# First softmax times values: four 32-column tiles of the matmul array, one for each batch and head

## Chip, core and metric

The kernel runs on one core of one Trainium2 chip, in one launch. The time is device microseconds of one execution; of several executions the median counts. The engines are named as in the profile: PE is TensorE's matmul, PEld its load of the stationary operand, DVE is VectorE, ACT is ScalarE, POOL is GpSimd, SP is the queue that issues most DMAs.

## The reference

Inputs are float32. Batch 8, heads 8, sequence 576, head width 64, 32 packed rows. `A` is the attention with the packed rows; what follows is a channel mixing block and a second one.

```
def sm_attn(qq, kk, vv):
    s = scale * np.matmul(qq, kk.transpose(0, 1, 3, 2))
    s = s - np.max(s, axis=-1, keepdims=True)
    a = np.exp(s)
    a = a / (np.sum(a, axis=-1, keepdims=True) + 1e-09)
    return np.matmul(a, vv)
p_packed = sm_attn(p, k, v)          # 32 rows a head
out = sm_attn(q, p_packed, p_packed) # 576 rows a head
...
k = np.maximum(xk @ w_k, 0.0); v = k * k @ w_v        # xk, xr: x mixed with the row before
r = 1.0 / (1.0 + np.exp(-(xr @ w_r))); x = r * v
...
u = x + (xt @ U @ V).transpose(0, 2, 1); return u + np.maximum(u @ w_ch1, 0.0) @ w_ch2
```

The change lies in the product `a @ v` of the first softmax, the last line of `sm_attn` in its first call.

## The kernel before

Attention is cut into 16 units: a unit is two batches (`b2`) by two heads (`h`), so four pairs of batch and head with 32 packed rows each, 128 rows in all. `attention_steps` writes one unit. Keys are turned (`kin` to `kh`), the packed rows are turned (`pbd` to `pT`), scores go to PSUM, `Exp` writes the unnormed weights to `a1` (512 columns for the first 512 keys, and 128 columns, block diagonal by batch, for the last 64). `a1` is turned into `at`, whose columns are the 128 packed rows in the order batch, head, row. `at` is then the stationary operand and the values `vin` stream: that is the product of the change. `pp` (the STT on DVE at L262) multiplies the result by the reciprocal sum `st[:, 9:10]` and by `hmask`, which keeps for each row the 64 columns of its own head and puts 0 in those of the other. `pp` is turned into `ppt` for the second softmax and copied to `ppz` for the last product; `xo` goes to HBM (`x_d`).

Before the change the product streams both heads' 128 value columns past a stationary tile of 64 columns (one batch, two heads): for each of four tiles of keys two matmuls, `b2` = 0 and 1, into PSUM partitions 0 to 63 and 64 to 127. The last 64 keys of both batches are one full 128 by 128 matmul. That makes nine matmuls a unit; half of what they compute is masked away. A float32 matmul runs as two passes, each with its own weight load, so the trace has 18 loads and 18 matmuls for a unit.

The program is not written in the order in which it runs. Every operation is added to `Plan`, with the operations it depends on; `Plan.emit` then runs through a model of the engines and puts each operation into its engine's queue when the model has it ready, by class (`cls`; attention has 0, the main blocks 1, weight casts 0, 1 or 3) and then by order of writing (PE, SP) or by time ready (others). Where an operation may run on ACT or DVE (`copy`, `square`), the model's clocks choose. The model's cost of a matmul is set in `mm` (L197): `f * max(f * n / 2.4, 107.0) + 3.0` nanoseconds with `f` = 2 for float32 and `n` streamed columns. The order is thus fixed at build time, and the engines run their queues in it.

Units 0 to 3 run first, interleaved by `LAG`, while the weights `w_r` and `w_k` are cast to pairs of rounded parts (`Cast.run`: on DVE per 128 by 512 block four full-width steps on `st`, `a`, `m`, one full-width split and two at double rate). Then twelve chunks of 384 columns follow; the other twelve units run beside the first of them, until 477 us. A chunk mixes (`mix`: ACT `m`, DVE `m`, `xr` or `xk`), multiplies (`psr`, `psk`, `psv`), and squares (`sq`, `kk`). The last part, from 752 us on, is the second block (`psc`).

Of the kernel before, what the change touches and what calls it, by code (L numbers as in the profile page):

```python
# [469 lines left out]
def packed_attention_moe_mixer_kernel(  # L470
# [18 lines left out]
    B, H, S, D = q.shape  # L489
    NP = p.shape[2]  # L490
    P = 128
# [16 lines left out]
    plan = Plan(nc)  # L508
    add, sub, mul = ALU.add, ALU.subtract, ALU.mult
# [22 lines left out]
    def ctile(name, shape, dt=F32):  # L532
        return plan.fixed(const.tile(shape, dt, name=name))

    ident = ctile("ident", [P, P])
    hmask = ctile("hmask", [P, 2, D])
# [8 lines left out]
    def ps_att():  # L545
        return plan.bank(att_banks[0], "psat", att_banks[0] is ps_a)
# [87 lines left out]
    def attention_steps(A, u, u_next):  # L634
        bp, j = divmod(u, NJ)
        kin, qin, vin = A.kin.pop(u), A.qin.pop(u), A.vin.pop(u)
# [5 lines left out]
        qt, at = A.big(F32, "qt"), A.big(F32, "at")  # L642
# [11 lines left out]
        for b2 in range(2):  # L654
            yield
            ps = ps_att()
# [6 lines left out]
        ps = ps_att()  # L663
# [10 lines left out]
        st = plan.tile(A.one, [P, 16], F32, "st", parts=(0, 1))  # L674
        sps = []
        for c in range(2):
            yield
            ps = ps_att()
            for b2 in range(2):
                plan.mm(ps[b2 * 64:(b2 + 1) * 64, 0:288], pT[:, b2, :],  # L680
                        kh[:, b2 * 576 + c * 288:b2 * 576 + (c + 1) * 288],
                        start=True, stop=True, skip_group_check=True)
# [16 lines left out]
        for c in range(3):  # L699
            yield  # L700
            ps = ps_att()
# [13 lines left out]
        ps = ps_att()  # L715
# [4 lines left out]
        ps = ps_att()  # L720
# [2 lines left out]

        yield
        ps = ps_att()
        vm = vin[:, 0:1024].rearrange("p (b h t d) -> p b h t d", b=2, h=2, t=4)
        for t in range(4):
            for b2 in range(2):
                plan.mm(ps[b2 * 64:(b2 + 1) * 64, 0:P],
                        at[:, t * P + b2 * 64:t * P + (b2 + 1) * 64], vm[:, b2, :, t, :],  # L730
                        start=(t == 0), stop=False, skip_group_check=True)
        plan.mm(ps[:, 0:P], at[:, 512:640], vin[:, 1024:1152], start=False, stop=True, skip_group_check=True)
        pp = plan.tile(A.one, [P, P], F32, "pp")
        plan.stt(pp, ps[:, 0:P], st[:, 9:10], hmask.rearrange("p h d -> p (h d)"), mul, mul)
        plan.copy(ppz[:, 0, :], pp)
        if not plain:
            plan.tt(ppz[:, 1, :], pp, ppz[:, 0, :], sub)
# [3 lines left out]
        ps = ps_att()  # L741
# [36 lines left out]
        ps = ps_att()  # L778
# [4 lines left out]
        ps = ps_att()  # L783
# [5 lines left out]
        for c0, c1 in ((256, 576), (0, 256)):  # L789
# [4 lines left out]
            for n, (lh, rh) in enumerate(terms):  # L794
                for b2 in range(2):
                    r = slice(b2 * 64, (b2 + 1) * 64)
                    plan.mm(pss[b2][:, 0:w], ppz[r, lh, :], rh[r, c0:c1], start=(n == 0),
                            stop=(n + 1 == len(terms)))
# [5 lines left out]
    def attention(A, u, u_next):  # L804
        for _ in attention_steps(A, u, u_next):
            pass
# [94 lines left out]
    plan.cls = 0  # L901
    A0.after = go
    steps = [attention_steps(AX_[u], u, NJ if u == 0 else None) for u in range(NJ)]
    step = 0
    while any(s is not None for s in steps):
# [301 lines left out]
    def product(q, f, i, name, fresh):  # L1207

        if fresh:
            bank_abc[name] = plan.bank(ps_c1, "psc1")  # L1210
        ps = bank_abc[name][:, 0:256]
        w, x = load_ws(f, i), ops[q][i]
        n = 0
        for k in range(2):
            for wi, a in PASS:
                plan.mm(ps, half(w, wi)[:, k * P:(k + 1) * P],
                        half(x, a)[:, k * 256:(k + 1) * 256],
                        start=(fresh and n == 0), stop=(n == 5), skip_group_check=True)
                n += 1
        return ps  # L1220
# [53 lines left out]
    for n in range(len(chunks)):  # L1274
        b, c = chunks[n]
# [59 lines left out]
    for q in range(NQ):  # L1335
# [11 lines left out]
        for f in range(NF):  # L1347
# [7 lines left out]
            b = product(q, f, 1, "b", True)  # L1355
# [71 lines left out]
```

## Time and profile before

| | |
|---|---|
| median of 3 runs | 1553.74 us (1549.9 to 1557.67) |
| profiled execution | 1553.02 us |
| its span, first to last instruction | 1551.2 us |
| PE busy | 1506.0 us, 97% of the span |
| DVE, ACT busy | 964.3 us, 705.0 us |
| mean granted TensorE clock | 0.986 |

The profiled execution's own time is 1.8 us longer than its span, which covers what lies before the first and after the last instruction. A busy PE is not yet PE at its peak: matmul records overlap, so the time that a kind of matmul costs is read from the distance between starts and not from one record's length. A granted clock of 1.00 is the level of 2.4 GHz, 0.50 that of 1.2 GHz.

### The profile page before, as it was taken

How to read it: one execution, taken by the hardware profiler on the slowest of the kernel's cores; microseconds unless marked ns; L12 is line 12 of the kernel's file. 1: busy time of each engine (PE TensorE's matmuls, PEld its weight loads, DVE VectorE, ACT ScalarE, POOL GpSimd, SP SyncE). 2: the span in 40 equal slices, each digit the busy share in tenths (PEclk: the TensorE clock that was granted, in tenths of full speed). 3: DMA queues.
4: the chain of work that ended last, by engine and by line, in shares of the span. 5: the costliest groups of instructions: out<-in, count | busy, mean ns of one | idle time of the engine just before them, and what ended most of it. 6: DMA issues, size and time to landing. Idle time of an engine off the chain costs nothing.

```text
span 1551.2 us, 24711 instructions
## 1 busy us (share of the span) xinstructions
PE 1506.0 (97%) x8836; PEld 1311.0 (85%) x8836; DVE 964.3 (62%) x2227; ACT 705.0 (45%) x1627; POOL 270.6 (17%) x522
## 2 busy tenths in 40 slices
PE   6879899999999999999999999999999999999998
PEld 5658687888878888888899998989999999999997
DVE  5988977788887776787645354444545454443533
ACT  4867576666675666566532232222222222222221
POOL 0000000000000000001133333333333333333331
PEclk8898999999999999999999999999999999999999
DMA  9866546465554323657777867686866768676763
GB/s 200 202 175 168 155 106 170 126 184 163 158 155 142 125 92 128 240 181 241 234 211 188 215 169 224 163 239 155 234 165 180 212 168 226 162 217 157 204 171 101
DMA packets 226745, 275.59 MB, mean 178 GB/s; under 512 B 101696, under 2 KB 120448, under 8 KB 226624
## 3 DMA queue, kind: packets, MB, share of 16 engines
q0 software_dynamic: 72576, 132.15, 32.5%
q1 hardware_dynamic: 154048, 141.87, 31.5%
q8 instruction: 71, 1.16, 0.3%
q14 instruction: 50, 0.41, 0.1%
HBM read 221.45 MB, written 52.50 MB: 177 GB/s over the span
## 4 chain that ended last, share of the span: by engine, by line
PE 91%; DMA 4%; DVE 2%; ACT 2%; SPq 1%; issue 1%; DVEq 0%; ACTq 0%
PE psc L197 48%; PE psk L197 13%; PE psv L197 12%; PE psr L197 6%; PE psat L197 5%; PE psat L208 3%; SPq L311 1%; PE psu L197 1%; PE psh L197 1%; PE pst L208 1%; DMA s<-w_d 1%; DMA st<-in_moe_w_k_dram 1%; ACT a L229 1%; DMA qin<-in_q_dram 1%; DMA x_d<-xo 0%
## 5 line engine op out<-in xcount | busy, mean ns | idle before, releaser
L197 PE MATMUL psc<-w,hid 128*128 128x512 f32 x1728 | 446.5, 393 | 0.0
L197 PEld LDWEIGHTS psc<-ob,wb 128*128 128x128 f32 x3024 | 406.9, 190 | 28.3 <-ACT tmp L280 1.6
L197 PE MATMUL psc<-ob,wb 128*128 128x256 f32 x3024 | 420.9, 283 | 1.3 <-ACT tmp L280 1.3
L311 POOL DMA_DIRECT2D wb<-ws_d x504 | 267.2, 530 | 586.9 <-PE psc L197 489.7
L197 PEld LDWEIGHTS psc<-w,hid 128*128 128x128 f32 x1728 | 305.9, 189 | 50.2 <-ACT xu L280 0.2
L197 PE MATMUL psk<-xk,wk 128*128 128x384 f32 x1152 | 235.2, 345 | 1.7 <-DVE xk L250 0.9
L197 PE MATMUL psv<-wv,kk 128*128 128x512 f32 x864 | 226.8, 399 | 3.0 <-DVE wv L250 2.1
L250 DVE TENSOR_TENSOR tmp<-tmp,psc 128x256 f32<-128x256 f32 x288 | 120.7, 419 | 152.3 <-PE psc L197 141.4
L197 PEld LDWEIGHTS psk<-xk,wk 128*128 128x128 f32 x1152 | 202.6, 190 | 13.6 <-issue 3.7
L229 ACT ACTIVATE hid<-tmp 128x256 fp32r<-128x256 f32 x216 | 85.2, 416 | 248.9 <-DVE tmp L250 248.6
L197 PEld LDWEIGHTS psv<-wv,kk 128*128 128x128 f32 x864 | 157.9, 188 | 36.9 <-issue 2.8
L265 DVE SCALAR_TENSOR_TENSOR hid<-psc,hid 128x256 fp32r<-128x256 f32 x72 | 30.5, 424 | 186.4 <-ACT hid L229 186.4
L197 PE MATMUL psr<-wr,xr 128*128 128x512 f32 x432 | 111.4, 401 | 6.2 <-ACT r L280 3.0
L280 ACT ACTIVATE tmp<-psc 128x256 f32<-128x256 f32 x144 | 54.7, 380 | 137.8 <-PE psc L197 137.8
L303 POOL MEMSET x<- 128x8 f32 x4 | 0.8, 206 | 576.2 <-DVE m L262 392.0
L197 PEld LDWEIGHTS psr<-wr,xr 128*128 128x128 f32 x432 | 79.5, 189 | 25.7 <-ACT r L280 3.9
L265 DVE SCALAR_TENSOR_TENSOR hid<-tmp,hid 128x256 fp32r<-128x256 f32 x216 | 86.2, 421 | 18.0 <-ACT hid L229 12.9
L250 DVE TENSOR_TENSOR kk<-sq,kk 128x384 fp32r<-128x384 f32 x96 | 52.5, 553 | 45.3 <-ACT kk L280 43.7
L229 ACT ACTIVATE sq<-psk 128x384 f32<-128x384 f32 x96 | 46.5, 489 | 64.4 <-PE psk L197 63.4
L229 ACT ACTIVATE hid<-psc 128x256 fp32r<-128x256 f32 x72 | 27.5, 382 | 103.6 <-PE psc L197 103.6
L229 ACT ACTIVATE m<-x,om_t 128x384 f32<-128x384 f32 x96 | 57.2, 609 | 7.0 <-DVE xk L250 2.8
L262 DVE SCALAR_TENSOR_TENSOR m<-x,mu_t,m 128x384 f32<-128x384 f32 x96 | 57.9, 610 | 2.1 <-ACT m L229 1.7
(147 smaller groups left out, 1685.9 us busy)
## 6 DMA issues: line engine op xcount, KB each, us to landing
wb<-ws_d POOLq DMA_DIRECT2D x504, 256.0 KB, 3.1
st<-in_moe_w_ch_dram SPq DMA_DIRECT2D x32, 512.0 KB, 4.9
ws_d<-wb SPq DMA_DIRECT2D x56, 256.0 KB, 3.4
qin<-in_q_dram SPq DMA_DIRECT2D x32, 288.0 KB, 5.6
x_d<-xo SPq DMA_DIRECT2D x16, 576.0 KB, 3.4
x_d<-x SPq DMA_DIRECT2D x36, 256.0 KB, 3.7
u<-x_d SPq DMA_DIRECT2D x36, 256.0 KB, 5.5
out_dram<-u SPq DMA_DIRECT2D x36, 256.0 KB, 3.6
```

Of the source, the lines that this page charges most:

```text
L197: self.nc.tensor.matmul(o, l, r, start=start, stop=stop, **k)
L208: self.nc.tensor.transpose(out.get(), in_.get(), ident.get())
L229: self.nc.scalar.activation(o, in_.get(), func, **k)
L250: return self.elem(engs, lambda e, o, x, y: e.tensor_tensor(out=o, in0=x, in1=y, op=op), out, [a, b], self.TT, cls)
L262: ("dve",), lambda e, o, x, y, z: e.scalar_tensor_tensor(out=o, in0=x, scalar=z, in1=y, op0=op0, op1=op1), out, [a, b, s], {"dve": (1.042, ...
L265: ("dve",), lambda e, o, x, y: e.scalar_tensor_tensor(out=o, in0=x, scalar=s, in1=y, op0=op0, op1=op1), out, [a, b], self.TT, cls)
L280: self.nc.scalar.activation(o, i, AF.Copy)
L303: (self.nc.gpsimd if eng == "pool" else self.nc.vector).memset(o, 0.0)
L311: (self.nc.sync if eng == "sp" else self.nc.gpsimd).dma_start(out=o, in_=i)
```

## The change

The product is now 20 matmuls a unit: for each of five tiles of keys (`t`; the fifth is the last 64 keys of both batches) four matmuls, one for each pair of batch and head (`g`). The stationary operand is 32 columns of `at`, the streamed one the 64 value columns of that batch and head, and the result goes to 32 PSUM partitions and 64 columns. `pp` then reads the 64 columns twice, by a broadcast, and masks as before.

```
-        vm = vin[:, 0:1024].rearrange("p (b h t d) -> p b h t d", b=2, h=2, t=4)
-        for t in range(4):
-            for b2 in range(2):
-                plan.mm(ps[b2 * 64:(b2 + 1) * 64, 0:P],
-                        at[:, t * P + b2 * 64:t * P + (b2 + 1) * 64], vm[:, b2, :, t, :],
-                        start=(t == 0), stop=False, skip_group_check=True)
-        plan.mm(ps[:, 0:P], at[:, 512:640], vin[:, 1024:1152], start=False, stop=True, skip_group_check=True)
+        for t in range(5):
+            for g in range(4):
+                o = t * P + g * 32
+                rhs = vin[:, g * 256 + t * D:g * 256 + (t + 1) * D] if t < 4 else \
+                    vin[:, 1024 + g % 2 * D:1024 + (g % 2 + 1) * D]
+                plan.mm(ps[g * 32:(g + 1) * 32, 0:D], at[:, o:o + 32], rhs,
+                        start=(t == 0), stop=(t == 4), skip_group_check=True)
         pp = plan.tile(A.one, [P, P], F32, "pp")
-        plan.stt(pp, ps[:, 0:P], st[:, 9:10], hmask.rearrange("p h d -> p (h d)"), mul, mul)
+        plan.stt(pp.rearrange("p (h d) -> p h d", h=2), ps[:, 0:D].unsqueeze(1).to_broadcast([P, 2, D]),
+                 st[:, 9:10], hmask, mul, mul)
```

The model of `Plan` has 217 ns for a float32 matmul of 128 columns and the same for one of 64, so the nine matmuls of a unit count 1.95 us there and the 20 count 4.34 us. With that the whole order moves. Two places show it.

On PE, in the first two units, the product (`vin,at`) stood in two pieces in unit 0, with the ninth matmul at the end of the second piece, and unit 1's product came later in one piece. Before:

```order
L208 MATMUL psat<-ident,a_151 128x128 x5
L197 MATMUL psat<-vin,at 64x128 x3
L208 MATMUL psat<-ident,qin 128x128 x6
L197 MATMUL psat<-vin,at 64x128 x5
L197 MATMUL psat<-vin,at 128x128
L208 MATMUL psat<-ident,qin 128x128 x3
L208 MATMUL psat<-ident,pp 128x128
L197 MATMUL psat<-ppt,qt 128x64 x8
```

Now, from the same place on as far as unit 1's product, which has three pieces:

```order
L197 MATMUL psat<-ppt,qt 128x128
L197 MATMUL psat<-vin,at 32x64
L197 MATMUL psat<-kh,pT 64x288 x4
L208 MATMUL psat<-ident,qin 128x128 x6
L197 MATMUL psat<-vin,at 32x64 x16
L208 MATMUL psat<-ident,kin 128x128 x4
L197 MATMUL psat<-vin,at 32x64 x3
```

Over the program the product stands in 18 pieces before and in 22 now; the four more are all in units 0 to 3, and from unit 4 on each unit's product is one piece.

On DVE, at the fourth unit's `pp`, the first mixing result of the first chunk (`xr`) stood five rows behind it, and the casts were then at the split of the second `w_k` block (`wk_0_182`). Before:

```order
L262 SCALAR_TENSOR_TENSOR m<-x,mu_t,m 128x384
L250 TENSOR_TENSOR m<-m,a 128x512
L262 SCALAR_TENSOR_TENSOR pp<-psat,st,hmask 128x128
L256 TENSOR_SCALAR a<-st 128x512
L269 TENSOR_REDUCE s_214<-a_720 128x16
L269 TENSOR_REDUCE s_214<-a_720 128x4
L283 COPY ppz<-pp 128x128
L250 TENSOR_TENSOR xr<-m,xr 128x384
L265 SCALAR_TENSOR_TENSOR a<-st,a 128x512
L256 TENSOR_SCALAR s_214<-s_214 128x16
L256 TENSOR_SCALAR s_214<-s_214 128x4
L250 TENSOR_TENSOR wk_0_182<-m,wk_0_182 128x512
```

Now the casts of all four such blocks stand ahead of that `xr`:

```order
L250 TENSOR_TENSOR wk_0_183<-m,wk_0_183 128x512
L262 SCALAR_TENSOR_TENSOR pp<-psat,st,hmask 128x128
L256 TENSOR_SCALAR st<-a 128x512
L283 COPY xo<-psat 128x4x64
L250 TENSOR_TENSOR m<-m,st 128x512
L283 COPY ppt<-psat 128x128
L250 TENSOR_TENSOR m<-m,a 128x512
L256 TENSOR_SCALAR om_t<-mu_t 128x8
L283 CAST wk_0_184<-m 128x512
L250 TENSOR_TENSOR wk_0_184<-m,wk_0_184 128x512
L262 SCALAR_TENSOR_TENSOR m<-x,mu_t,m 128x384
L265 SCALAR_TENSOR_TENSOR st<-a,st 128x512
```

Counted in DVE's queue, cast steps at full width (STT and TT of 128 by 512) and at double rate (TENSOR_SCALAR of 128 by 512) stand ahead of the first `pp` 7 and 3 before, 9 and 4 now; ahead of the fourth `pp` 30 and 12, now 37 and 15; ahead of the first `kk` of the first chunk 60 and 24, now 68 and 28. Over the whole program 22 copies went from ACT to DVE. POOL's queue is the same.

## Rows read from the trace of the kernel before

**Rows 1.** Page, busy time and share of the span by engine.

```profile
PE 1506.0 (97%) x8836; PEld 1311.0 (85%) x8836; DVE 964.3 (62%) x2227; ACT 705.0 (45%) x1627; POOL 270.6 (17%) x522
```

**Rows 2.** Page, forty equal slices: busy tenths, granted clock.

```profile
PE   6879899999999999999999999999999999999998
DVE  5988977788887776787645354444545454443533
PEclk8898999999999999999999999999999999999999
```

**Rows 3.** Windows: stretch, length, PE, PEld, DVE, ACT, POOL busy, clock, DMA, GB/s.

```profile
64.00:110.00 46.00, 37.15 (x188) 27.64 (x187) 39.62 (x99) 31.73 (x76) 0.00 (x0) 0.85 0.73 188
110.00:160.00 50.00, 46.27 (x265) 38.22 (x265) 44.31 (x108) 36.06 (x88) 0.00 (x0) 0.90 0.66 172
160.00:225.00 65.00, 58.19 (x337) 45.93 (x336) 53.63 (x136) 41.80 (x101) 0.00 (x0) 1.00 0.53 130
225.00:290.00 65.00, 64.25 (x376) 52.49 (x375) 50.72 (x125) 44.76 (x103) 0.40 (x1) 1.00 0.56 156
560.00:1560.00 1000.00, 984.94 (x5909) 885.35 (x5907) 514.37 (x1147) 335.66 (x773) 268.66 (x509) 1.00 0.67 188
```

**Rows 4.** Waits of PE, 110 to 225 us: us, times, longest.

```profile
PE psv L197 <- DVE wv L250: 2.1, 1, 2.1
...
PE psk L197 <- DVE xk L250: 0.9, 2, 0.7
PE psk L197 <- ACT xk L280: 0.8, 1, 0.8
```

**Rows 5.** The product's matmuls (tile vin on PE) by stage: length, busy, clock, DMA.

```profile
0.00:64.00 64.00, 8.35 (x72) 0.87 0.88 196
64.00:110.00 46.00, 1.51 (x18) 0.85 0.73 188
110.00:160.00 50.00, 3.02 (x36) 0.90 0.66 172
```

**Rows 6.** Timeline, unit 1's product: start, length, engine, operation.

```profile
38.53 0.49 PE L208 MATMUL psat<-ident,qin 128*128 128x128 f32 x3
...
38.95 0.85 PEld L197 LDWEIGHTS psat<-vin,at 128*64 128x64 f32 x16 [0.17 <-issue]
38.95 1.51 PE L197 MATMUL psat<-vin,at 128*64 128x128 f32 x18
...
39.98 0.30 PEld L197 LDWEIGHTS psat<-vin,at 128*128 128x128 f32 x2 [0.17 <-DVE st L269]
...
40.30 0.49 PE L208 MATMUL psat<-ident,qin 128*128 128x128 f32 x3
```

**Rows 7.** Lines by form: line, engine, operation, shapes, count; busy, mean ns; idle before.

```profile
L197 PE MATMUL psat<-vin,at 128*64 128x128 f32 x256 | 19.5, 293 | 2.6 <-ACT at L280 2.6
```

**Rows 8.** Windows of PE in unit 1's product: busy, records alive, clock, DMA, GB/s.

```profile
39.54:39.65 0.11, 0.11 (x6) 1.00 1.29 268
...
40.08:40.19 0.11, 0.11 (x1) 1.00 1.33 228
```

**Rows 9.** The same view at the lower clock, in unit 0's product.

```profile
26.90:27.11 0.21, 0.21 (x6) 0.50 1.06 410
```

**Rows 10.** Timeline, 64 streamed columns against 128 stationary ones, and what follows.

```profile
126.41 2.17 PE L197 MATMUL psat<-ppt,qt 128*128 128x64 f32 x18
128.33 0.71 PE L197 MATMUL psv<-wv,kk 128*128 128x512 f32 x2
```

**Rows 11.** Lines by form: DVE's cast steps, full width and double rate, and `pp`.

```profile
L265 DVE SCALAR_TENSOR_TENSOR st<-a,st 128x512 f32<-128x512 f32 x52 | 35.4, 686 | 8.8 <-ACT a L229 8.7
...
L256 DVE TENSOR_SCALAR st<-a 128x512 int32<-128x512 int32 x52 | 21.4, 421 | 0.1
...
L262 DVE SCALAR_TENSOR_TENSOR pp<-psat,st,hmask 128x128 f32<-128x128 f32 x16 | 5.6, 347 | 5.9 <-PE psat L197 5.8
...
L250 DVE TENSOR_TENSOR pbd<-p,hmask 128x128 f32<-128x128 f32 x16 | 4.3, 284 | 5.7 <-DMA p<-in_p_dram 4.7 <-PE psat L208 0.9
```

## Prediction, written before the changed kernel ran

> **What bounds the kernel now.** I read the page's busy shares first: PE 97% of the span, DVE 62%, ACT 45% [rows 1]. The forty slices then show that this is not one regime [rows 2]: PE has slices of 6 to 9 at the left end and of 9 to the right of it, and DVE and the granted clock are the other way round. The windows by stage put numbers to it [rows 3]. From 225 us on PE is busy 64.25 of 65 us and later 985 of 1000 us at clock 1.00: there a microsecond of PE work is a microsecond of time. From 64 to 110 us PE is busy only 37.15 of 46 us while DVE is at 39.62 of 46, and the clock is 0.85; from 110 to 225 us PE leaves 3.7 and 6.8 us idle, and its waits name what DVE and ACT deliver: the last step of a cast of `wv` for 2.1 us, `xk` for 0.9 and 0.8 us [rows 4]. So up to some 160 us the casts, the mixing and the attention on DVE set the pace about as much as PE does. The product of the change lies in both regimes: of its 288 matmul records 72, 18 and 36 are before 160 us [rows 5], which is 7 units at 18 records, and 9 units come after.
>
> **What a unit's product costs now.** In unit 1, at the full clock, its first matmul starts at 38.95 us and the next kind of work at 40.30 [rows 6]: 1.35 us. The 16 narrow records fill 38.95 to 39.98, when the load for the 128-wide matmul starts: 1.03 us. A narrow record is 293 ns long in the mean [rows 7] and six are alive at once [rows 8], so two start in every 0.1 us: the two batches' tiles run side by side. In the 128-wide matmul one or two are alive. At the clock of 0.50 the same six are alive in a stretch of 0.21 us [rows 9], so a round of two doubles with the clock, which says that the streamed columns set it: 0.109 us at the full clock for 128 columns in one pass. Eight rounds are 0.87 us, and 1.03 less 0.87 leaves 0.16 us for the first load and for emptying the array at the end. The 128-wide pair has 0.32 us, of which two rounds are 0.22 and 0.10 is a load that nothing hides.
>
> **What it will cost.** Half the columns make a round of 0.055 us (an estimate from the 0.109). The loads don't stop that: a stationary tile of 128 columns with 64 streamed ones takes, for its 18 records (the last two with 128 columns), from 126.41 to 128.33 us, 0.107 us each [rows 10], so the load is what it waits for, and 32 columns of load are a quarter, 0.027 us. If all four tiles run side by side, five tiles of keys in two passes are 10 rounds, 0.55 us. The 0.16 and the 0.10 stay, since the array still has to be filled and left: 0.81 us against 1.35, a saving of 0.54 us a unit. The bounds are wide, because no row has four tiles at once. The low end of the cost is 0.81; the high end is that 40 records start one after the other at the mean distance of the 16 that we have, 1.03 / 16 = 0.064 us: 2.56 + 0.26 = 2.82 us, a loss of 1.47 us. I take the low end, because two tiles share a round without lengthening it, and that at both clocks [rows 8, 9].
>
> The Trainium skill speaks against this choice: its page "TensorE: Matmul & The Clock Gate", section "Wait — 56ns, not 53.3ns?", states that with hardware decode off the sequencer spends about 62 ns on each matmul however small it is. By that, as an estimate, 40 matmuls would take 2.48 us and not 0.55, a loss of some 1.4 us a unit. Our 0.064 us a record neither agrees nor disagrees, since a burst of 16 may have been queued beforehand, and no run here shows a longer one.
>
> **The sum on PE.** 16 units at 0.54 us are 8.6 us. Two of the early products lie mostly in stretches at the lower clock, where two thirds of the saving doubles: 2 x 0.36 = 0.7 us more. Four more pieces (18 to 22, all in units 0 to 3) cost an entry and an exit each: 38.53 to 38.95 us is 0.42 us for three transposes of 0.109 [rows 6], so 0.09 for the entry, and 0.16 + 0.10 for the exit, 0.35 us a piece, 1.4 us in all. PE's work falls by 7.9 us. Of this the 9 units after 160 us have 9 x 0.54 = 4.9 us, which is kept where PE has no idle time, and the early part has 3.0 us, of which little is kept if DVE sets the pace.
>
> **What the new order costs.** The operations on DVE are the same, but the planner now counts 4.34 us for a unit's product instead of 1.95 and lets casts go ahead. Up to the first `kk` of the first chunk DVE's queue has 8 full-width cast steps and 4 at double rate more. At 686 and 421 ns [rows 11] that is 5.5 + 1.7 = 7.2 us more work ahead of the first squares, and PE's `psv` cannot start without them. It is not lost work: these casts are those of `w_k` and `w_v` that stood behind. The ends: 7.2 us later if DVE is the pace all the way; 3.8 us earlier if the waits for `wv` and `xk` (2.1 + 0.9 + 0.8) vanish, because the casts are done. PE's idle time from 110 to 225 us is 3.7 + 6.8 = 10.5 us, in which a late start can be made up; I take half of it as made up, 5.2 us, and so a cost of 7.2 - 5.2 = 2.0 us.
>
> **What costs nothing.** `pp` writes as many elements as before, and reads 64 columns twice. A DVE operation on the same shape with a broadcast operand has 284 ns and `pp` 347 [rows 11], so 0.06 us either way, times 16 at most 1 us on an engine with 38% to spare; in the early part, 7 x 0.06, it is 0.4. 22 copies more on DVE and fewer on ACT lie mainly where both are under 70% busy; were they early, at some 0.5 us each, they would be part of the 7.2 above. 352 more loads and matmuls in the program are fetched beside the run, and no wait of PE in the rows is for its own instructions. The second half, from 560 us on, has the same work; PE idles 15 of 1000 us there, so nothing is to be had or lost.
>
> **The forecast.** 1553.0 of the profiled execution less 4.9 plus 2.0 is 1550.1 us. The median stands 0.7 us above that execution, so 1551 us for the median. Its own range is 1547 to 1555.
>
> **Rivals.** All are for the median.
> First, the early part gains too. An early unit's product stands between two steps on DVE, and partly at the lower clock, where it is twice as long. If the 3.0 us are kept and DVE's order costs nothing or wins the 3.8 back, the time is 1553.7 - 7.9 = 1545.8 down to 1542.0; 1544 in the middle. For it speaks that PE has work for 37 of the 46 us from 64 to 110, close to DVE's 40; against it that DVE is busy 86% of them [rows 3].
> Second, slower by the order. The place is the first chunk's start, 64 to 160 us. If the 7.2 us stay whole, because DVE goes on at 44.31 of 50 us from 110 to 160 [rows 3], and PE, waiting more, is granted the lower clock for one more stretch like the 0.50 ones here (some 6.8 us, costing half of that, 3.4), the time is 1553.7 - 4.9 + 7.2 + 3.4 = 1559.4. It decides from the point at which the delay of the first `psv` exceeds 4.9 us.
> Third, the change doesn't do what it says: only two of the four tiles run side by side, as now. Then 20 rounds of 0.055 make 1.1 + 0.26 = 1.36 us, no saving, and 1.4 of pieces and 2.0 of order stay: 1557.
> Fourth, every record costs its own 0.064 us. The 9 late units lose 9 x 1.47 = 13.2 us, all 16 lose 23.5: with the 2.0 of the order 1569 to 1579, 1573 in the middle. The rule named above would end here as well.
>
> **How the numbers follow.** Chances: forecast 0.36, first rival 0.26, second 0.24, third 0.06, fourth 0.08. A measurement of this kernel can tell about 0.5%, 7.8 us, from no change, so faster means below 1546 and slower above 1561.5. Below 1546 lies most of the first rival and a little of the forecast, 0.22; above 1561.5 lie the fourth and a part of the second, 0.18; the rest, 0.60, is within. The range takes in the first rival's end and the second: 1541 to 1562 leaves out the fourth and a tail at each end, 0.2 in all.
>
> **What would show it.** In the changed profile a unit's product in one piece should take from its first matmul to the next kind of work 0.8 us (third rival 1.35, fourth 2.8), and at the full clock more than six records should be alive in 0.11 us. The windows after 225 us should hold the same idle time as now. The start of the first `psk` and of the first `psv` tell forecast, first and second rival apart: later by some 2 us, earlier, or later by 7 with more 0.50 in the clock. The waits for `wv` and `xk` between 110 and 225 us should shrink. I am wrong if the distance to before is not made of these two things, the 9 late units and the first chunk's start: for instance if PE shows new waits after 225 us because the other queues' order no longer fits a product that is four times shorter than the planner counts.

## The result, and the profile after

The changed kernel took 1568.61 us, the median of 6 runs (1565.56 to 1574.3), against 1554.08 us for 6 runs of the kernel before (1549.9 to 1557.67): a ratio of 1.0094, 95% interval 1.007 to 1.0119. It is slower by 14.5 us. The forecast was 1551, and its range ended at 1562. The profiled execution after took 1574.3 us with a span of 1572.5, against a span of 1551.2 before; it is the slowest of the six, 5.7 us above their median.

The page of the changed kernel, busy time and the slices that answer to [rows 1, 2]:

```profile
PE 1514.2 (96%) x9188; PEld 1312.3 (83%) x9188; DVE 976.9 (62%) x2249; ACT 698.0 (44%) x1605; POOL 269.4 (17%) x522
...
PE   6879899999999999999999999999999999999998
...
PEclk8689899999999999999999999999999999999999
```

PE is busy 8.2 us longer, though its product became shorter. That is the clock: slice 2 went from 8 to 6, slices 3 and 5 from 9 to 8, and only slice 4 from 8 to 9. The windows by stage of the changed kernel, columns as in [rows 3]:

```profile
64.00:110.00 46.00, 32.78 (x206) 22.07 (x205) 39.47 (x95) 26.44 (x67) 0.00 (x0) 0.72 0.81 201
110.00:160.00 50.00, 47.94 (x289) 38.74 (x287) 43.32 (x105) 39.76 (x89) 0.00 (x0) 0.97 0.48 135
160.00:225.00 65.00, 56.10 (x339) 43.80 (x338) 52.21 (x133) 35.85 (x85) 0.00 (x0) 0.87 0.52 134
225.00:290.00 65.00, 63.03 (x422) 51.51 (x421) 49.96 (x123) 40.54 (x93) 0.11 (x1) 1.00 0.50 138
...
560.00:1560.00 1000.00, 999.81 (x5980) 899.31 (x5979) 528.46 (x1170) 347.36 (x794) 267.89 (x509) 1.00 0.68 190
```

Against [rows 3], PE is busy 4.4 us less from 64 to 110 us, at 0.72 instead of 0.85; 110 to 160 is better; from 160 to 225 it is busy 2.1 us less at 0.87 instead of 1.00, and from 225 to 290 1.2 us less. What PE waits for in the whole span (us, times, longest), before and then after:

```profile
PE psat L208 <- DMA kin<-in_k_dram: 5.6, 2, 4.3
...
PE psat L208 <- DVE pp L262: 2.2, 2, 1.3
...
PE psat L208 <- DVE a L250: 1.0, 1, 1.0
```

```profile
PE psat L208 <- DVE pp L262: 20.5, 12, 5.5
PE psat L208 <- DMA kin<-in_k_dram: 6.8, 4, 4.5
PE psat L208 <- DVE a L250: 5.6, 2, 3.2
```

The row that grew most is that of `pp`: PE stands before the turning of `pp`, the step behind the changed product, 12 times instead of twice and 18.3 us longer. The turning of `a` waits 4.6 us longer. The timeline of the changed kernel at one late unit shows why (start, length, engine, operation; in brackets the idle time before):

```profile
355.67 0.77 PE L197 MATMUL psat<-vin,at 128*32 128x64 f32 x40
...
356.37 1.42 PE L197 MATMUL psv<-wv,kk 128*128 128x512 f32 x5
356.44 0.69 DVE L250 TENSOR_TENSOR m<-m,st 128x512 f32<-128x512 f32 x1
...
357.33 0.56 DVE L250 TENSOR_TENSOR kk<-sq,kk 128x384 fp32r<-128x384 f32 x1 [0.20 <-ACT kk L280]
...
357.81 0.68 DVE L250 TENSOR_TENSOR m<-m,a 128x512 f32<-128x512 f32 x1
358.41 0.68 DVE L265 SCALAR_TENSOR_TENSOR st<-a,st 128x512 f32<-128x512 f32 x1
...
359.13 0.43 DVE L256 TENSOR_SCALAR a<-st 128x512 int32<-128x512 int32 x1
359.47 0.35 DVE L262 SCALAR_TENSOR_TENSOR pp<-psat,st,hmask 128x128 f32<-128x128 f32 x1
...
359.87 0.33 PE L208 MATMUL psat<-ident,pp 128*128 128x128 f32 x1 [2.08 <-DVE pp L262]
```

The product is over 0.70 us after it began: the next kind of work starts at 356.37. But the planner had counted 4.34 us for it, so in DVE's queue it put four cast steps and a `kk` ahead of `pp`, some 3 us of work, and in PE's queue only as much behind the product as filled the rest of that plan. On the chip PE is through at 357.79 and stands 2.08 us. From the product's start to the turning of `pp` it takes 4.20 us here, and 2.74 at the same unit of the kernel before (361.92 to 364.66 us in its timeline).

### The profile page after: what moved, and what is told of

Its sections match the earlier page's. It is cut to its first block, busy times and chain, and to the rows that moved or that the text cites. A ratio compares the mean times of both kernels' runs of the same rounds, so it can differ in the third digit from the quotient of the medians.

```text
span 1572.5 us, 25392 instructions
## 1 busy us (share of the span) xinstructions
PE 1514.2 (96%) x9188; PEld 1312.3 (83%) x9188; DVE 976.9 (62%) x2249; ACT 698.0 (44%) x1605; POOL 269.4 (17%) x522
## 4 chain that ended last, share of the span: by engine, by line
PE 68%; DMA 0%; DVE 0%; issue 0%; ACT 0%; DVEq 0%; ACTq 0%
PE psc L197 47%; PE psv L197 7%; PE psk L197 7%; PE psr L197 3%; PE psh L197 1%; PE pst L208 1%; PE psat L197 1%; PE psu L197 1%; DMA s<-w_d 0%; PE psat L208 0%; DVE u L250 0%; DVE w L250 0%; DVE x L250 0%; DVE tmp L250 0%; DVE m L250 0%
## 5 line engine op out<-in xcount | busy, mean ns | idle before, releaser
L197 PE MATMUL psv<-wv,kk 128*128 128x512 f32 x864 | 233.0, 403 | 0.8 <-DVE wv L250 0.5
L265 DVE SCALAR_TENSOR_TENSOR hid<-psc,hid 128x256 fp32r<-128x256 f32 x72 | 30.5, 423 | 184.6 <-ACT hid L229 184.6
L280 ACT ACTIVATE tmp<-psc 128x256 f32<-128x256 f32 x144 | 54.7, 380 | 138.5 <-PE psc L197 138.5
```

Source lines behind the costliest of these rows:

```text
L197: self.nc.tensor.matmul(o, l, r, start=start, stop=stop, **k)
L265: ("dve",), lambda e, o, x, y: e.scalar_tensor_tensor(out=o, in0=x, scalar=s, in1=y, op0=op0, op1=op1), out, [a, b], self.TT, cls)
L280: self.nc.scalar.activation(o, i, AF.Copy)
```

## The experiments

All but two change numbers in the planner, so that the same operations stand in another order, with some copies on DVE instead of ACT or the other way round (29 fewer on DVE in e1 than in the changed kernel). "Booked" is what the planner counts for a unit's product; "four tiles" is the changed product, "wide" the old one. The table is worked out from the records of each profiled execution: **early** runs from the first matmul to the second chunk's first `psv`, **middle** from there to the eighth chunk's first `psr` (the expectations call these two chunk 2 and chunk 7), **idle** is PE's time without a matmul in both together, **low** the time at 0.50 in both. What comes after the middle has 1010 to 1014 us in all but e9 (1016.5) and e13 (1021.7). Each ratio is to the kernel before as it was measured beside that run.

| run | median us | ratio to before (95%) | early | middle | idle | low |
|---|---|---|---|---|---|---|
| before: wide, 1.95 us | 1554.08 | | 203.3 | 326.7 | 34.6 | 41.0 |
| after: four tiles, 4.34 | 1568.61 | 1.0094 (1.007 to 1.0119) | 203.6 | 349.2 | 49.1 | 81.9 |
| e1: four tiles, 0.61 | 1545.2 | 0.9937 (0.9918 to 0.9957) | 204.2 | 320.2 | 35.4 | 58.0 |
| e2: four tiles, 1.95 | 1552.9 | 0.9979 (0.9963 to 0.9994) | 208.9 | 322.1 | 41.1 | 51.2 |
| e3: wide, 4.34 | 1581.71 | 1.0166 (1.0135 to 1.0196) | 214.4 | 346.2 | 54.7 | 68.2 |
| e4: wide, 1.09 | 1549.51 | 0.9972 (0.9961 to 0.9983) | 200.2 | 327.8 | 33.8 | 47.8 |
| e5: four tiles, 0.61; 3.73 elsewhere | 1582.14 | 1.0187 (1.0172 to 1.0202) | 207.7 | 352.4 | 63.2 | 75.1 |
| e6: four tiles, 3.0 | 1550.76 | 0.9972 (0.9959 to 0.9985) | 199.3 | 329.1 | 41.9 | 51.2 |
| e7: four tiles, 1.2 | 1552.99 | 0.9991 (0.9976 to 1.0006) | 212.6 | 320.3 | 44.3 | 61.4 |
| e9: after, `pp` planned later | 1568.01 | 1.0082 (1.006 to 1.0103) | 196.1 | 343.2 | 50.8 | 58.1 |
| e13: after, main work booked 8% less | 1575.79 | 1.0132 (1.0097 to 1.0166) | 202.6 | 334.9 | 46.3 | 64.9 |
| e14: four tiles, 3.0, main work booked longer | 1556.59 | 1.0008 (0.9988 to 1.0028) | 204.9 | 332.2 | 51.1 | 58.1 |

The middle has the products of 8 units in every row but that of e9 (9), so no product went to another stretch by the change. Other steps of a unit did: at full clock (busy time, with that at 0.50 halved) the early part has 152.5 us of PE's work before and 140.5 after, the middle 323.8 and 326.6, and the tiles save less than 5 us in each.

### The tiles or the booking: e1 to e4

One theory: the booked time makes the order, and the order makes the waits. The rival: the four tiles themselves cost more than their records show. e1 and e2 keep the four tiles and change the booking alone (e2 also counts as many columns for the planner's model of the clock as before; its order then differs from that before in the product's own rows only). e3 and e4 keep the wide product and change its booking alone.

```
 e1, in mm():
-            return f * max(f * n / 2.4, 107.0) + 3.0
+            return 30.5 if l.shape[-1] == 32 else f * max(f * n / 2.4, 107.0) + 3.0
 e2, in mm():
-            self.cols = f * f * n * r.shape[0] / 128.0
-            return f * max(f * n / 2.4, 107.0) + 3.0
+            self.cols = 4608.0 / 20 if l.shape[-1] == 32 else f * f * n * r.shape[0] / 128.0
+            return 1953.0 / 20 if l.shape[-1] == 32 else f * max(f * n / 2.4, 107.0) + 3.0
 e3, the kernel before (e4: 109.0 for the first eight, 217.0 for the ninth):
-            return f * max(f * n / 2.4, 107.0) + 3.0
+            return book or f * max(f * n / 2.4, 107.0) + 3.0
...
-        plan.mm(ps[:, 0:P], at[:, 512:640], vin[:, 1024:1152], start=False, stop=True, skip_group_check=True)
+        plan.mm(ps[:, 0:P], at[:, 512:640], vin[:, 1024:1152], start=False, stop=True, skip_group_check=True, book=4340.0 / 9)
```

> The changed product, but the planner counts each of its 20 matmuls 30.5 ns, 0.61 us a unit, near the 0.77 us that the changed kernel's trace shows. Booking theory (the planner's 4.34 us let other DVE work in between the product and pp, so that PE waits): the 20.5 us that PE waited for pp fall below 4 us, the extra stretches at the clock of 0.50 go with them, and the time is 1540 to 1550 us. Tile theory (the 32-column tiles themselves slow PE or lower its clock): 1562 us or more, whatever the planner counts. Chance theory (any new order moves the time by some 10 us either way): anywhere from 1540 to 1565 us, without a tie to the wait for pp.

> The changed product, but the planner counts the unit as it counted the nine matmuls before, 1.95 us in all, so that nearly every queue has the order of the kernel before. Only the tiles change. Booking theory: PE's wait for pp stays near the 2.2 us of before, each unit's product is some 0.5 us shorter, and the time is 1545 to 1550 us. Tile theory: 1560 us or more, with the clock's low stretches of the changed kernel. Chance theory: 1545 to 1550 us as well, since the order is not new.

> The product of before, nine matmuls, but the planner counts 4.34 us for it. Booking theory: the loss shows without the tiles; PE waits for pp for 10 to 20 us and the time is 1565 to 1580 us. Tile theory: 1550 to 1557 us, no change. Chance theory: 1544 to 1564 us.

> The product of before, but the planner counts what the trace shows, 109 ns for each narrow matmul and 217 for the wide one, 1.09 us a unit. Booking theory: the 1.95 us were already 0.6 to 0.9 us too much, so a small gain, 1545 to 1553 us. Tile theory: 1550 to 1557 us. Chance theory: 1544 to 1564 us.

e1 took 1545.2 us, 23.4 less than the changed kernel with the same operations, and less than the kernel before. e3 took 1581.71, 27 more than the kernel before with the same operations. So the booking is worth more than the whole change, and the tiles by themselves lose nothing; the rival falls. In e3 the wait stands at the same place (waits of PE):

```profile
PE psat L208 <- DVE pp L262: 22.6, 13, 4.7
```

In e1 it is 2.0 us, and the timeline of e1 at a late unit shows `pp` next in DVE's queue when the product is done, with nothing in between:

```profile
366.63 0.77 PE L197 MATMUL psat<-vin,at 128*32 128x64 f32 x40
...
367.33 1.19 PE L197 MATMUL psv<-wv,kk 128*128 128x512 f32 x4
367.47 0.35 DVE L262 SCALAR_TENSOR_TENSOR pp<-psat,st,hmask 128x128 f32<-128x128 f32 x1 [0.49 <-PE psat L197]
...
367.87 0.69 DVE L250 TENSOR_TENSOR x<-psv,r 128x512 f32<-128x512 f32 x1
...
368.60 0.27 PE L208 MATMUL psat<-ident,pp 128*128 128x128 f32 x1
```

Here DVE waits for PE (0.49 us) and PE for nobody: 1.97 us from the product to the turned `pp`.

e2 is the tile alone, at before's order: 1552.9 us against 1554.67 for the kernel before, where 1545 to 1550 was expected; the interval of the ratio is 0.9 to 5.8 us less. The middle is 4.6 us shorter, but the early part 5.6 longer in its profiled execution: 4.3 us less work there, 7.0 more idle time and 2.9 more from the lower clock (half of the busy time at 0.50). The timeline of e2 in unit 1 shows one place where the gain went:

```profile
37.29 0.77 PE L197 MATMUL psat<-vin,at 128*32 128x64 f32 x40
37.98 0.55 PE L208 MATMUL psat<-ident,qin 128*128 128x128 f32 x3
41.62 0.61 PE L208 MATMUL psat<-ident,kin 128*128 128x128 f32 x2 [3.09 <-DMA kin<-in_k_dram]
```

Before, unit 1's product began at 38.95 and the same `kin` was turned from 40.81 us on, without a wait. PE gets there sooner, the transfer doesn't, and PE's wait for `kin` grows from 5.6 to 9.8 us in the whole span. e4, with a nearer booking of the wide product, is 0.3% faster too (1549.51), but in its profiled execution (1553.04) the middle is no shorter.

### How much of an excess is too much: e6 and e7

The booking is moved between the true 0.61 and 4.34 us: 150.0 (3.0 us) and 60.0 (1.2 us) in place of 30.5.

```
 e6, over e1 (e7: 60.0):
-            return 30.5 if l.shape[-1] == 32 else f * max(f * n / 2.4, 107.0) + 3.0
+            return 150.0 if l.shape[-1] == 32 else f * max(f * n / 2.4, 107.0) + 3.0
```

> The changed product counted 3.0 us a unit (150 ns each). Booking theory: between the runs at 1.95 us (1552.9) and 4.34 us (1568.6), 1557 to 1564 us, with a wait of PE for pp between 4.2 and 20.5 us, near 11. Chance theory: no order among the runs; below 1553 or above 1568 as likely as between.

> The changed product counted 1.2 us a unit (60 ns each). Booking theory: between 1545.2 (0.61 us) and 1552.9 (1.95 us), 1545 to 1552 us, wait of PE for pp 2 to 4 us. Chance theory: outside of that as likely as inside.

The middle follows the booking without exception: 320.2 us at 0.61, 320.3 at 1.2, 322.1 at 1.95, 329.1 at 3.0, 349.2 at 4.34. At 3.0 and 4.34 some 4 to 7 us of that is work that stood in the early part at the other bookings; idle time and lower clock alone cost the middle 0.5, 1.6, 2.4, 5.0 and 22.5 us. PE's wait for `pp` from 200 us on follows the booking too: none in e1, 4.0 us in e6, 11.3 in the changed kernel. The whole time does not follow it: e7 took 1552.99 and e6 1550.76, both outside of what the booking theory expected, since the early part lies anywhere between 199 and 213 us. Each booking makes another order there, and nothing that was tried ties its length to the booking.

### Is it the place behind the product: e5 and e9

One theory says that the waits come wherever the planner counts too much, a rival that the chain product, `pp`, turning is special. e5 books the product truly and adds the missing 3.73 us to the last matmul of a unit's last product, whose reader is the copy `xo`. e9 keeps the booking of 4.34 and tells the planner that `pp` ends 3.73 us later than it does, so that PE's queue gets other work before the turning.

```
 e5, over e1:
-            return 30.5 if l.shape[-1] == 32 else f * max(f * n / 2.4, 107.0) + 3.0
+            return 30.5 if l.shape[-1] == 32 else f * max(f * n / 2.4, 107.0) + 3.0 + more
...
-                            stop=(n + 1 == len(terms)))
+                            stop=(n + 1 == len(terms)), more=3730.0 * (c0 == 0 and n + 1 == len(terms) and b2 == 1))
 e9, over the changed kernel:
-                op.fin = t + dur
+                op.fin = t + dur + op.late
...
-                  st[:, 9:10], hmask, mul, mul)
+                  st[:, 9:10], hmask, mul, mul).late = 3730.0
```

> The changed product counted 0.61 us as in e1, and the 3.73 us that the changed kernel counts too much put on the last product of the same unit (ppz times th, whose result nobody on PE waits for soon). The planner thinks PE as busy as in the changed kernel. Place theory (the loss comes from DVE work planned between the product and pp): PE waits for pp 2 to 4 us in all, and the time is 1543 to 1553 us. Total theory (any PE time counted too much misplaces work for the other engines everywhere): 1560 us or more.

> The changed kernel with its booking of 4.34 us a unit kept, but the planner takes pp's result to come 3.73 us later, so that it puts other PE work ahead of the transpose that waits for pp. The DVE work between the product and pp stays. Waiting theory (the loss from chunk 2 to chunk 7 is PE standing at that transpose): PE's wait for pp falls from 20.5 to below 6 us, the stretch from the first psv of chunk 2 to the first psr of chunk 7 (349 us in the changed kernel, 327 before, 320 in e1) falls to 320 to 332 us, and the time is 1545 to 1556 us. Rival (the order as a whole is bad at that booking, the wait is a sign of it only): the stretch stays above 340 us and the time above 1562 us.

e5 took 1582.14 us, worse than the changed kernel, as the total theory has it. PE's waits in e5, whole span:

```profile
PE psat L208 <- DVE xo L283: 9.3, 5, 2.8
...
PE psat L208 <- ACT xo L280: 7.4, 9, 2.3
...
PE psat L208 <- DVE pp L262: 3.2, 4, 1.6
```

The kernel before has no such row for L208 at `xo`. The wait moved to the reader of the matmul that is booked too long, and waits elsewhere grew with it: it follows the excess, and the product is not special. In e9 the wait for `pp` is down to 3.6 us, but the time is 1568.01, as in the changed kernel. Its waits:

```profile
PE psat L208 <- DMA kin<-in_k_dram: 9.5, 5, 4.4
PE psr L197 <- ACT xr L280: 7.3, 3, 4.5
PE psat L208 <- DMA qin<-in_q_dram: 6.3, 4, 1.9
```

PE's idle time is the same (50.8 against 49.1 us) under other names. So the row of 20.5 us names where the misfit shows, not what it costs: to move that one wait out of the way gives nothing back.

### Does the same order repeat: e10 and e11

The changed kernel and the kernel before once more, unchanged, each with a profile.

> The changed kernel once more, for a second trace. Stretch theory: from the first psv of chunk 2 to the first psr of chunk 7 again 345 to 353 us (349 in the first trace), and the early part, up to that psv, 199 to 210 us (204). If both differ by as much as between kernels, one trace a kernel is too little to tell the bookings apart.

> The kernel before once more, for a second trace. Stretch theory: from the first psv of chunk 2 to the first psr of chunk 7 again 323 to 330 us (327), while the early part, 203 us in the first trace, may differ by 5 us from one execution to the next, since e2 with nearly the same order had 209.

They took 1566.39 and 1553.44 us. The early part repeats within 0.2 us (203.4 and 203.1), so as far as two traces each can show it the 5 us by which orders differ there are the orders' and not chance; I had expected more spread. The middle of the kernel before repeats too (326.6), that of the changed kernel doesn't: 341.3 against 349.2, with the same 12.3 us idle, but 3.4 instead of 20.5 us at 0.50. Where these come from can be seen in the changed kernel's first profile. Three waits of the timeline, and then the windows of PE around them (busy, clock, DMA, GB/s):

```profile
210.43 0.33 PE L208 MATMUL psat<-ident,pp 128*128 128x128 f32 x1 [1.73 <-DVE pp L262]
...
396.09 0.33 PE L208 MATMUL psat<-ident,pp 128*128 128x128 f32 x1 [1.89 <-DVE pp L262]
...
476.64 0.33 PE L208 MATMUL psat<-ident,pp 128*128 128x128 f32 x1 [1.91 <-DVE pp L262]
```

```profile
205.80:212.60 6.80, 5.08 (x65) 0.97 0.01 2
212.60:219.40 6.80, 6.80 (x26) 0.53 0.48 155
219.40:226.20 6.80, 6.80 (x37) 1.00 0.04 10
...
389.40:396.20 6.80, 4.91 (x66) 1.00 1.02 243
396.20:403.00 6.80, 6.80 (x29) 0.52 0.52 101
403.00:409.80 6.80, 6.80 (x36) 0.97 0.00 0
471.00:477.80 6.80, 4.89 (x61) 1.00 0.41 123
477.80:484.60 6.80, 6.80 (x30) 0.55 1.09 253
484.60:491.40 6.80, 6.80 (x36) 0.95 0.43 147
```

Behind each of these waits the granted clock is at the lower of its two levels for one stretch in which PE is busy throughout: some 3.4 us more, after a wait of 1.7 to 1.9. Behind the waits of 2.08 us (at 359.87) and 1.76 us (at 437.79) it stayed at 1.00, and the kernel before has no stretch at 0.50 from 143 us to the end of PE's work. The second execution of the changed kernel has the same five waits, 1.73 to 2.08 us long, and only behind that of 1.89 us a stretch of 3.4 us at 0.50. So a wait can cost nearly three times its length, but doesn't always, and its length doesn't say when.

### A plan that runs faster than the chip: e13 and e14

The planner counts 216 ns for a main matmul of 512 columns (512 / 2.4 + 3), and 24 of them take 5.44 us in the kernel before, from the first start to the next kind of work (539.12 to 544.56 us), 227 ns each. A theory: the chip's PE falls behind its plan by that, and the lag swallows part of the product's excess, which is why 3.0 us does so little. Then less booked for the main work should shrink the waits (e13), and more should grow them (e14).

```
 e13, over the changed kernel:
-            return f * max(f * n / 2.4, 107.0) + 3.0
+            return (f * max(f * n / 2.4, 107.0) + 3.0) * (0.92 if f == 1 else 1.0)
 e14, over e6:
-            return 150.0 if l.shape[-1] == 32 else f * max(f * n / 2.4, 107.0) + 3.0
+            return 150.0 if l.shape[-1] == 32 else f * max(f * n / 2.4, 107.0) + (3.0 if f == 2 else 14.0 if n < 512 else 18.0)
```

> The changed kernel with its 4.34 us for the product kept, and the main blocks' matmuls counted 8% less than before (199 ns for 512 columns, where the trace has 231). Lag theory (PE waits where the planner's PE, over a unit's period of some 37 us, is slower than the real one: the main matmuls, counted 7% short, let the real PE fall behind by some 2 us a period, the product counted 3.6 us too long takes that up and 1.5 us more): now the real PE falls behind by some 4.5 us a period, more than 3.6, so the idle time of PE from chunk 2 to chunk 7 falls from 12.3 to below 5 us, that stretch from 349 and 341 to 320 to 328 us, and the time is 1543 to 1557 us. Product theory (only the product's own booking counts): the stretch stays above 340 us and the time above 1562 us.

> The product counted 3.0 us as in e6 (1550.8 us), and the main matmuls counted as the trace shows them, as in e12 (1551.9 us). Lag theory: nothing takes up the 2.2 us that the product is counted too long, so PE idles 8 us or more from chunk 2 to chunk 7 (e6: 5.0, e12: 2.7), the stretch is 334 us or more (329, 319) and the time 1557 to 1575 us. Product theory: as e6, 1547 to 1554 us.

The direction came out: the wait for `pp` went from 20.5 to 13.6 us in e13, and from 10.2 in e6 to 16.5 in e14, which is 5.8 us slower than e6. The sizes fell short: in e13 PE's idle time in the middle went from 12.3 to 10.9 us only, where less than 5 was expected, and e14 has 7.4 us of it where 8 was expected. e13 as a whole is slower than the changed kernel (1575.79), with 1021.7 us after the middle. So the lag is a part of it at most, and why the loss grows so steeply between 3.0 and 4.34 us stays open.

### Is there more to win: e8 and e12

Both are e1 with a further booking brought nearer to the trace: e8 halves that of the float32 matmuls on tiles of 64, which run in pairs; e12 books the main work longer, as in e14.

```
 e8, over e1:
-            return 30.5 if l.shape[-1] == 32 else f * max(f * n / 2.4, 107.0) + 3.0
+            return 30.5 if l.shape[-1] == 32 else f * max(f * n / 2.4, 107.0) / (2 if f == 2 and min(l.shape) == 64 else 1) + 3.0
 e12, over e1:
-            return 30.5 if l.shape[-1] == 32 else f * max(f * n / 2.4, 107.0) + 3.0
+            return 30.5 if l.shape[-1] == 32 else f * max(f * n / 2.4, 107.0) + (3.0 if f == 2 else 14.0 if n < 512 else 18.0)
```

> As e1, and the other float32 products that run two at once (kh times pT, and ppz times th of the plain units) counted half as long too, as the trace shows them. Booking theory: another small gain over e1, 1540 to 1546 us. Chance theory: 1538 to 1553 us.

> As e1, and the matmuls of the main blocks counted as the trace shows them (120, 174 and 231 ns for 256, 384 and 512 columns, where the planner has 110, 163 and 216). Booking theory: the planner's PE is then no faster than the real one, waits stay as in e1, 1541 to 1548 us. Chance theory: 1538 to 1555 us.

They took 1549.91 us (0.997, 0.9956 to 0.9984) and 1551.85 us (0.9981, 0.9964 to 0.9998), above what the booking theory expected of each. Their middles are the best of all (318.0 and 319.1 us), their early parts are 211.1 and 209.7 us, and so both are behind e1. e1, at 1545.2 us, is the best version found: the change with the product booked at 0.61 us.

## Why the prediction was wrong, by its steps

**The tiles: right.** Four tiles do run side by side. In the changed kernel a unit's product takes 0.70 us from its first matmul to the next kind of work, where 0.81 was forecast and 1.35 measured in unit 1 before (1.27 in the late units). Windows of PE in that product, to be read as [rows 8]:

```profile
355.78:355.89 0.11, 0.11 (x16) 1.00 1.66 359
...
356.00:356.11 0.11, 0.11 (x24) 1.00 0.88 191
```

16 and 24 records are alive in 0.11 us, where six were. In the records of this product the four tiles start 6 to 7 ns apart, and a round of four 56 ns after the one before it, where 0.055 us was forecast. PE's matmul work at the full clock (busy time, with that at 0.50 halved) fell from 1486.9 to 1477.7 us, by 9.2; the forecast was 7.9. Third and fourth rival fall with that. Each of the 40 records costs 0.70 / 40 = 18 ns here, not 64. The rule in the Trainium skill's "TensorE: Matmul & The Clock Gate", section "Wait — 56ns, not 53.3ns?", of some 62 ns for each matmul with hardware decode off would make 2.48 us of it, as an estimate. This trace has 0.70 us; no run shows how decode was set.

**What the early units keep: right in sign.** The forecast let the late units keep their gain and the early ones lose theirs. e2, the tile alone, has just that: 4.6 us less in the middle, and nothing left of the early units, since PE idles there instead, at the one place shown for a transfer. But the early part then costs 5.6 us more there, so the tile alone is worth 1.8 us by the medians (3.3 by the ratio) and not 4.9. The first rival, that the early units gain too, did not come about.

**What the new order costs: the step that failed.** It was sized at 2.0 us, from one place, the casts ahead of the first `kk`. The part where that place lies is as long as before, 203.6 us against 203.3, but by coincidence: it has 12.2 us more of idle time and lower clock (36.8 and 26.3 against 31.7 and 19.2) and 12.0 us less work, some 7 of which now stand in the middle. Of the 12.2 us, 9.9 come with the tile alone, since e2 has 38.7 and 22.1 there. The order itself costs in the middle, where the forecast had PE without idle time: 9.4 us more idle, 10.2 from the lower clock and 2.9 more work make its 22.5 us. Of its 12.3 us idle, 11.3 are at the `pp` behind the product, which the planner had put up to some 3 us too late in DVE's queue; by e9, to end that wait alone gives nothing back. Measured against the same tiles at the order before, the order costs 1568.6 - 1552.9 = 15.7 us; against e1's booking it is 23.4, of which not all is the booking's, since e7, with the same middle as e1, is 7.8 us slower by its early part alone. In the two profiles, from first to last matmul: 9.2 us less work, 13.4 us more idle time of PE (49.3 against 35.9), and 17.3 us more from the lower clock (half of the busy time at 0.50: 36.5 against 19.2), which gives the 21.5 us between the two executions (1563.5 against 1542.0). The median of all runs differs by 14.5, and the second profiles of both kernels differ by 7.9 from the clock in place of 17.3.

**The second rival: right in its sign and in part of its mechanism.** It forecast 1559.4 from a late start of the first chunk and one more stretch at the lower clock. The first `psv` was later by 3.6 us, but the second chunk's was not, and of the waits for `wv` and `xk` [rows 4] 0.5 us is left. The lower clock did cost 7.1 us more in the early part, 2.9 of them with the tile alone. But the larger part of the order's loss came after 208 us. The last sentence of the prediction named this course, new waits after 225 us because the other queues' order no longer fits, and gave it neither a price nor a chance. A bound of its price could have been read: the planner's 4.34 us against the forecast 0.81 is up to 3.5 us of other engines' work ahead of `pp` in each of 16 units.

**What costs nothing: right.** From 560 us on PE idled 0.2 us in 1000 (of the 15 us in [rows 3], which the prediction took for idle time, 8.8 lie behind the end of that span and 4.9 behind PE's last matmul), and the part after the middle took 1010.8 us against 1011.9.

## What to carry to other kernels

Where a static order comes from a model of the engines, an operation's new time must go into the model with the operation: the same tiles took 1568.6 us at the old formula and 1545.2 at 0.61 us booked. How near the booking must be is not shown: 1.2 us took 1553.0 and 3.0 us 1550.8. A change of shape changes the order through its cost, so price every place where the order puts other engines' work between the changed operation and its reader, once for each time it runs, and not only the first. To tell the two apart, run the new shape at the old booking and the old shape at the new one; and don't chase the one wait that the profile names, since the idle time can return under other names.

## What the runs showed of the hardware that was not expected

40 matmul records on four column tiles of 32, ten rounds, took 0.70 us at the full clock, the first load and the emptying included, though a float32 matmul is two passes. And of five waits of PE of 1.73 to 2.08 us in the middle of dense work three were followed by 6.8 us at the lower of the two clock levels, and two, of 1.76 and 2.08 us, were not; the same order in a second execution had the same waits and 3.4 us of it instead of 20.5.
